# Two more input slots for the first batch, borrowed from tiles that are idle then, and a new order table

## The chip, the cores and the metric

The kernel runs on one core of one Trainium2 chip. The metric is device time in microseconds, the median of the runs shown. One execution was also taken by the hardware profiler; lines and durations in this text come from it.

## The reference

Two layers stand one behind the other, on four batches of 6272 steps and 256 channels.

```python
sig = 1 / (1 + exp(-f_logit))
f = lower_bound + (1 - lower_bound) * sig
for t in range(S):                       # S = 6272
    h = f[:, t] * h + (1 - f[:, t]) * x[:, t]
    y[:, t] = h
proj = y @ w_proj                        # 256 -> 3 * 256: x1, x2, x3
x2_conv = irfft(rfft(x2) * rfft(filter_fft))     # along t, circular, length S
out = (x1 * x2_conv * x3) @ w_out
```

The first is a gated recurrence, the second a long convolution between two gates. The filter's spectrum is the same for all batches and is made once.

## The kernel before

**An order written out.** No instruction is issued where the source names it. `op(...)` records an operation with the engines it may run on; `ORDER`, a table of packed entries, gives for each step the operation, its engine and its PSUM bank. `emit` goes through the table and issues. So the order on every engine, which engine evacuates what, and whether the third projection is copied or multiplied directly (`MUL`) all stand in the table. SP issues every DMA, in its table order: a DMA that waits holds back those behind it.

**Preparation (`prepare`).** The filter comes in 13 loads (`ff`, L610) of four rows each. A copy rounds them (`fr`, to a double buffer `afs`; ScalarE, GpSimd or VectorE), TensorE rotates them (`rot`, L621), and 26 evacuations (`f2`) write the filter's own layout. Meanwhile VectorE works out sine arguments (`args`), ScalarE takes two sines, and tables are cut from them. Then the filter's DFT: 32 matmul groups (`FF1`, L646) evacuated as `afs`, 16 groups (`FF2`, L664) evacuated as `hw` into a staging place, one last group (`last`) for the self-conjugate lines. From the staging place two DMAs for each pair of units (`hst`, L673; `hst2` and `hst3` are those of pair 1) store the spectrum in HBM. `hws` is the ring of places: three in `Hu`, two in `A`, two in `PP`, seven pairs' worth, for eight pairs.

**The recurrence (`hgrn`).** Thirteen chunks of 512 steps. A chunk's gate and input are loaded into slots of `FL` and `XT`, NX = 3 of each, in turn (`load`, L321). ScalarE takes a sigmoid (`sig`, L324), GpSimd multiplies (`u`, L326), TensorE turns both in two halves (`su`, L338), ScalarE or VectorE makes the gate (`f`, L351 or L353), VectorE scans (`scan`, L359). The first 3072 steps are copied behind the sequence as well (`wrap`, L293), since the convolution is circular.

**The rest.** `P` (L705) projects x2 once all scans and wraps of its batch are there. `F1`, `F2`, a product with the spectrum (`prod`, `pm`) and `I2` go through 16 units, four at a time. The gate (`x13`, L387, evacuated by `xs`) runs among them. At the end of a batch `I1`, `y`, `proj`, `o` and `store` make the output, with the next batch's recurrence among them. Some matmuls use 64 rows of the array (`su`, `F2`, `mini`, `I1`, `FF2`, `last`), the others 128.

**Places that the change touches.** `A` is 4096 columns of `HA`: scratch for the sine arguments at first, a staging place of the filter's spectrum next, and from the first `F1` on the ring of the DFT of the batches. `x1s` and `x3s` hold the gate's projections from the first `x13` on.

Of the kernel before, what the change touches and what calls it, by code (L numbers as in the profile page):

```python
# [9 lines left out]
F32 = mybir.dt.float32  # L10
# [49 lines left out]
class Plan:  # L60
# [63 lines left out]
    "AAYABIACIAOYA0gA5gA+gBIgBDgA1ABNgBSgBXgBcgBhgAxQAeQAhQAoQAcQAzYArQAPIAbQA6YBrgBmgA2QA4IA3AAQAA/YAmSBASBwgBJAA7UB"  # L124
    "BCBCCA8EAwWAlQD6gA9EBEYBFQBOYBGABKSBTYBMCARIBPUBQEBYIAUIBUWBdYBVOBRED5gBHIAqUASAADgBWGBZUBiYBaMBbEAkWBeWBLCEFgBj"
    "QBkABfGAWIATIERgBgGBlABsIAsSBnIBtSBoUEGgAVYAXYAYYAZYBxAB1YB2YBuCAfQByQB0ABzABvCBpMBqMB3QB4IB5SB+UB6KB7YD7AD8YCJQ"
    "B8SEHACOWB/MCAUCBECKIB9KCHQCIIETAESgCDUD9SCEMAFgCCYCPGCLYEBQCQWAEYD+CD/KECAEdgEIYCRGCSYEegEUYEDICMUCTWCNECUGEJSA"
    "aYEKKENUEOEEpgEqgELKEPMCZQCaACgWEVQEZSE1gEaKAHAE2gChGEbKCXWAIAEfAEgYCeUEWACYGCbYEXICcWAJACfECdOCiYCjSErAEsYEhQEl"
    "UFBgCkCEiIFCgEjIEmECuWALAEnMCvGE3AAnSCpSAMACqKEtQExWEuAFLgEvICnUE4YEyGFMgEzOCoECrYCwSGHgCsUCxCCyYFDAE5QE6IE9SE+K"
    "FVgFEYC5WE7IFWgCtEAKAEEYC6GC3UC4EEYYE/KCzWFNAFFUFIQFfgFJIC0GDASFGEFOYFKIFHMDBCC+WC/GC7YDCYC8SFggFXAFYYFPWFQOFROF"  # L130
    "SQFpgFqgDJUEcYC9CE0YFTAFUIDDSDKEDECDHUFhAFiYDIEDLYFZWFaOFbOFcSFzgF0gDQQFdCDRAFeKDOUDPEDSYCGgDMQDNIDTUFrAFsYCFgFj"
    "WEwYDUEFkGFlODeSDfCFmUAGgDXQF1AF2YF9gDYADZSDaCDbYFnMFoMDgWEQYDhGDiYFtQDcSFuAFvIF+gFwWDdCDGgMegFxGFyODpUDqEF3SF4C"
    "F5KDjQDkADwUDxMF6WF/AGAYF7GF8ODuQDvADnSDoCDrYDyYDFgGBUGCEEoYGDMDzQD0ADsSEkYCVgANAEAYC1gDtCDWgE8YClgGEWD3UGIgEMAG"
    "FOGGOMgAJbQJcRJgWJiGJdIJepJfYD4MJhXJlQJmRD1gJjPJoBJnIFAYGZSGaCGfUGgMGTWGUGGNQGOAJkYGPSD2gGQKGbUGXQGVSGJWGcMMqgGL"
    "UGYAGKGJpYMsAGRQCmgCWgGSAGWKGMMGdSGeCDmgC2gJqUJrVJsMJttJuYGhQGiAGtgJvWJwXJxOJyPJzYGjQGkAGnSGoCJ0UGlVJ2MGmNDlgJ1Q"
    "J5RJ3AJ4YGuSJ6QDVgGyqGzYG2gJ7BJ8AJ9YGwqGpUGqEJ+RKABJ/QKDTGxYGrUGsMGvYKFDG3WG7GG5uHRRKBoHSBKCYG/gKETG0UG1EKGrKHYH"
    "AWHCGHTQG8YHUAMfgHXUHEuHFYHJSG6YG4YHYEHIgG9WG+GHNqHOYHDYHVQHWAHKYKIUKJVHLqKNWKPGHBYKLNKOTKQDMrgHbgHGQMhYHZWHaOHc"
    "SHgqHeqHfYHMYKKEHHAHhYHlUHnEHkgKMYH/WIAGHdYHPQHmYHpsHoYHQAKSTKUDKRYKTUKVsIDWHuQIEGHiSHjCIBUICEHqYKXWKZGKYXHtgHyo"
    "HzYHwoHvYHxYMtYH2gKavKbYHrSH4YHsCIJgH3UH7sH5sH6YIFQIGAH0WM2gH1GH8YIKSIHQIIIILYIOCIMqKcVINYKeFITWIXGM4AKdTISgKfrH"
    "9QIPYH+AKhXIUYKjHIVuIbgItUIuEIWYIYYKiSKmTKoLIQQIRAIcWIeGKkqMiUIguM3gIkgIhYIlQMjEIpAMmSMnCMkMIdYI3gMoKIfYIZWIaGIm"  # L140
    "YInoKnRKppKqYNCgIqYJAgIvUIwENDgIiWIjGIxSIyCKlYMuUM5YMvMMwMIzWI0GIoYMyQNOgNPgNEAI4SI1WI2OI8CJBUKWYI5YI6qI7YMzAI9Y"
    "IrWJCYJJgNFYKrTKsSJSgJDEKtDM0IKwUIsGJFsJGYKyEKxTKzrKuqM6QM7AM8IM+WNagM/GK0YI+UI/EJEYK1TK3LK2SNQAJTUNRYNbgNGQJVEK"
    "6TNHANAOK7UJLYK8DNKWK4qK9sK+YKvYJXENIINLGJHSJYYJICJUYK/ULBELAVK5YLCFLDYNmgKgYNcANMOJKQJOoJPYNSSNngNWUNwgLEWNTCJM"
    "oLGGNdYJNYNXENUKNxgLFXLJRLLBLKWNoANpYLMuLNYLHvLIYNYMJQQLOSLPTJRALQCLRrLSYNeWNfGNgONZYNiQNjAN6gN7gLTSLVCLUULYVLZT"
    "R7SLWsJWYNyALXYNkILaFNqWNtUR9CNzYOEgLbrLcYNrGNsONuENvMR8SR+COFgJZQSATSBSJaALdQLeISDCSCDLiWN0UN3SOOgN8AN9YN4CM9AN"
    "JYLjOOPgN1EN5KN2MLfQOGAOHYLnWLoOLkSLgALhgMpYLlCLmgLsULtMN+QOBWOYgM1YLxSN/AOAIOCGODOOQAORYLpULqELrgOZgLuQLvALwgL2"
    "ULyKL3MOIWOJGOLQOigOjgOKOOMALzSL0CL1gONIOSUL7WL8OOTENBYOUMMlYOaAOVSOWCOXKL4QL5AL6gNVYNhgL9WMAUMBML+GL/gMFQMGIObY"
    "OcSOdCOeKOkAOfWOgGOhOU+gMCUOlYMxYMHQVKgMDEMEgOmSOnCOoKOpUOqEOrMVWgMPWMQOVXgNlAMIAMJgMKSMLKNNYOyUOzMO2QO3IU/gOwWO"
    "xGO4SO5KPAUPBMOsWO+QO/IVAAO8SO9KVMAOtGPCUPDMO6QO7AO0WO1OVYAOuSOvCVZYMMQPEUPFMMNAMOgMUWMVOMZSPGUPHEMRQMSAMaKSEYPK"
    "WPLOPQUPUsPVYPMSPNCVLgPSsPTYPogPIQPJAMWWSFSSGTMXGMYgPYQR/YSIDSHKPOUPPMPRYPcoPdYSJYPpWPgSPaoPbYPrGSKUP7gPiCPxVPZY"  # L150
    "SMEPWRPjYPkqPlYPhYPyFSLUSNsSPQPeVPsYPtuPuYPqYPXBSRAPfFQEgPzRP0BSQQSUTSSoSWLP1UP2EPmWPnGSVQSXoMTgP3RP4BQNgP8UPvWQ"
    "AsPwGVBYSYYP5QP6IP9YQGYP+sSOYP/YQFSQHCSZVQBYSbFQOWQSGQfQQgASaSQIYQJqQCUQTYQPYQXQQbASeTSfXSgDSjRQWgScqSlBQhSQiCQp"
    "gSdYQDMQQuQRYQKYSTYQLUQYYQcYQMESkRShvQjWQkGSmpQygQZoQaYQUSQqUQusQvYVNYSoRQVCSqBQssQtYQlWQmGQdSQeCSpQStRSroSsYSvB"
    "QnWQoOQ0YQrYQzUQ1sQ2YQ7gQ8SQ3EQ4YRFQREgQ+CRACSuVSwtQwWQ/YRBYQxGRJIRNSROKRXgVCUVGWVDEVjgVEMSyRVigVHGS0BVFgSzSS3TS"
    "4RSxYQ5UVIOS1CQ9YS5DS6BRggRPSQ6ERQCRHoS2YRIYVOWRKYVPOVQOSnYRRURSERCQS7YRYSRcqRDARpgS8URaqS+ERGYS9VS/FTAYRTQRUAVS"
    "WVvgVugVTGRhURVQRWIRdYRygRZYTBSVkAVlYTDCTCTTEDVUORLQTFYRlsRqWRMARuGRjsRmYVJgVaSRbYVbCVcKRkYReQRvYRfATGXVeUVmQV6g"
    "TIHRsuV7gRtYRiYVfEVgMVnAVoITHSTJCTLTTNDVqWWHgWGgVwARnSVrGTMUTOsRrYTKYRoCTQVTSFVxYTRQTVRTWSTTATUYV8AV9YVsOVhYRwUR"
    "zWTXJTYqSiYR1uRxEVyQV2SWQgVzAV0IWRgV3CV4KR3uR4YTaUTcETbVTfWTdFThGTgUTeYR2YV+QWCVWbgTZYTiETjYV/AWagV5gTkUTlSTpTR0"
    "YTqXWIAWJYTmEWAITnqTrDTsvTtYWDFV1gTuUTwER5QWENTvSTzTTxqTyYR6AT0UT4XToYT1DT2EMbQMcIMdgT5WT6HVdgT3YT9UWKQWLAWNSWOC"
    "WSAWTYTPYWkgT7uT8YT+MUCWUDOWPKT/UWlgWcAWdYWMIUAEUBgUEWUFGUHSUIKUGgUMUUNMWUQWVAWWIWXWWvgWYGWZOUJSWugUOUWmAUKCULgU"  # L160
    "RQUSIUPEWeSWhWWBYWnYVRYWfCWgKW4gWiGWjOW5gVtYabUadEacVUTQaeFUUAUWSUXKUbUUcMWwAWxYWoWWrQXDgWsAWtIagSahTaiCUYUWpGWq"
    "OajDW6AUgQUhIWySWzCUQgW0KVpYUZEUdWUlQUmIUVgUagW1UW2EW3MXCgUiSUqQUrIW7YUeGUfgVVgW8WUjCW/UdqgW9GW+OdegXAEXBMdrgXEA"
    "UnSWFYXFYUoCUsQXGWXHGXIOXJSXKCXLKd3gUkgUvUUwMUtAU0WU1OXOSXPCXMQXNIdfgdsAdtYXQUXRMXkSXlKdgAXaWXbOXcQXdIXUUXVEXiSX"
    "jKUugdhYXgWXhGXWQXXIXeUXfMXSSXTCXYQXZAUxWU5SU6KafYUpgd2gUyGUzgXsQXtAXoUXmSXpMakYXnCXqWXrOalQamRanAU2UaopapYXuSXv"
    "KX5YXxYd4AU3EU4gX4WX8uX9YXwQXyoXzYX0AX1YaqSYIgasCarTatDauYavRaxBX6uX7YYbgdiUdjEYTSYUCdkMdmQeDgeCgYAWdnAX2SYCuYDY"
    "YEGYFYX+UYKYYkgdoIX3CYBYX/EawXYRSYSCayva0Wa2OazYduUdyQdvEdzAa1Sa5TdwMa3Cd0Ia7DYGWYHGYVSYWCa4YYJUYLsYMYeOgYXWYYGd"
    "5YYNsYOYYtga6Qa+RbABa/SbBqbCYbDTYcWa8Aa9YYZQYaIYdYd6UeEAYeGYfYd7EYguYhYd8MbESbGCY2gYPQYmYbIWbJXbFDbHYbLPYQAbKGY/"
    "SYlUbMYYnsd+QZACeagYuWd/AYoYYyGYiSYvYYjCYzYbNUbOXbPEYpsZJgbQHYwuYxYePgZSgZBSZCCYqYYrUY4YYsEeAIY3WY7uY8YdlYZDSZEC"
    "Y5uZbgY0QY1AZFUdpYY6YeBgebgbRYbSXbUPbTSbVqbWYeFYd1YZGEY9QZHUZIMZLYZUYZKWZOOZPYZMuZkgZNYZTSZVqZWYZvUY+AeQAZwEZXqZ"
    "3gbXQbYRbcXZYYbZAeGUbeHbaBbdQbbYeHEbfAeIMZcWZQRZdYZgubgYZeGZfYaAgZhYZRBbhQbiTbjAbmWbnSecAbkrblYboGbpqbqYZtQZZUZm"  # L170
    "YedYZuAbrXbsWbuGZlSbtHbvYZaMZnqZzQZ0AZxUZyEZiWZpqaJgZ4QZoYZqYbwSZ8oZjGeRYbyCbxTbzDZ1UZ2MZ5YZ6oZ7YZ9YeKWemgaKReLG"
# [22 lines left out]
def kernel(  # L194
# [51 lines left out]

    FF1 = [("FF1", u, h) for u in range(NU) for h in range(2)]
    FF2 = [("FF2", u) for u in range(NU)] + ["FF2"]
    late = {}
    dram = ctx.enter_context(tc.tile_pool(name="dram", bufs=1, space=bass.MemoryType.DRAM))  # L250

    H = [dram.tile([2, M + 64, 2 * UE * 64], F16, name=f"H{u}") for u in range(NU // 2)]
# [695 lines left out]
```

## Time and profile before

| | |
|---|---|
| median of 3 runs | 465.07 us (464.01 to 465.59) |
| profiled execution | 461.81 us, span 460.0 us, granted clock 0.996 |
| first sigmoid, last sigmoid of batch 0 | starts at 25.70, ends at 69.56 us |
| last scan of batch 0 | ends at 73.04 us |
| first P of batches 0 to 3 | 75.2, 172.4, 273.4, 372.1 us |
| loads, stores | 121.67 MB, 264 GB/s over the span |

A stage boundary here is the start of the first matmul of line L705 in each batch. Busy shares are of one execution. Matmuls are pipelined, so a busy TensorE needn't be at its peak.

### The profile page before, as it was taken

What the parts mean: (1) busy time and instruction counts of PE and PEld (TensorE: products, weight loads), DVE (VectorE), ACT (ScalarE), POOL (GpSimd) and SP (SyncE); (2) the same over time, 40 slices, a digit from 0 to 9 for tenths busy, and PEclk for the clock granted to TensorE, in tenths of its full rate; (3) what the DMA queues carried; (4) which work ended last, traced back from release to release, by engine and by line L of the source; (5) the groups of instructions that cost most, each with busy time, mean ns of one, the idle gap of its engine ahead of it and who ended that gap; (6) DMA issues with size and microseconds to landing.
All of it is one profiled execution on the core that took longest, in us unless ns stands there. A gap on an engine that the chain in (4) does not pass through costs nothing.

```text
span 460.0 us, 14639 instructions
## 1 busy us (share of the span) xinstructions
PE 440.7 (96%) x6009; PEld 345.1 (75%) x6009; DVE 412.9 (90%) x472; ACT 399.7 (87%) x578; POOL 317.3 (69%) x299
## 2 busy tenths in 40 slices
PE   7798999999899999999999999999999999999998
PEld 5676778777766889777767889776768897777786
DVE  8689998789999999999999998999999957999972
ACT  4899998799899986889998985999999887899564
POOL 7698875197899840689997624689996522889600
PEclk9899999999999999999999999999999999999999
DMA  8978999877988897586887977578677832567276
GB/s 326 398 271 288 328 303 341 290 247 264 339 287 273 292 312 279 162 259 217 313 314 282 349 259 292 209 256 285 234 271 254 330 140 93 185 184 210 79 295 268
DMA packets 44531, 121.67 MB, mean 264 GB/s; under 512 B 4272, under 2 KB 6960, under 8 KB 44464
## 3 DMA queue, kind: packets, MB, share of 16 engines
q1 hardware_dynamic: 44464, 120.73, 74.6%
q8 instruction: 47, 0.77, 0.7%
q14 instruction: 20, 0.16, 0.1%
HBM read 87.69 MB, written 31.98 MB: 260 GB/s over the span
## 4 chain that ended last, share of the span: by engine, by line
PE 51%; DVE 12%; ACT 2%; issue 1%; DVEq 0%; ACTq 0%
PE PS L387 13%; PE PS L817 7%; PE PS L869 7%; PE PS L705 6%; DVE HA L359 5%; DVE ys L857 5%; PE PS L777 5%; PE PS L718 5%; PE PS L338 4%; PE PS L851 3%; DVE X L286 2%; PE PS L591 1%; ACT HA L281 1%; PE PS L734 0%; ACT Th L281 0%
## 5 line engine op out<-in xcount | busy, mean ns | idle before, releaser
L326 POOL TENSOR_TENSOR XT<-XT,FL 128x1024 f32<-128x1024 f32 (+1 forms) x52 | 116.9, 2250 | 55.6 <-ACT FL L324 40.6
L359 DVE TENSOR_TENSOR_SCAN HA<-fTs,HA,PS 128x512 f16<-128x512 f32 (+1 forms) x96 | 112.5, 1200 | 3.8 <-ACT fTs L351 3.3
L798 DVE TENSOR_TENSOR PP<-PS,Hu 98x1008 f16<-98x1008 f32 x87 | 101.4, 1197 | 3.8 <-PE PS L817 1.5
L387 PE MATMUL PS<-HA,W 128*128 128x490 f16 (+1 forms) x416 | 101.0, 367 | 1.2 <-ACT HA L281 1.1
L807 POOL TENSOR_TENSOR PP<-HA,Hu 98x1008 f16<-98x1008 f16 x41 | 86.2, 2108 | 3.4 <-ACT HA L281 3.2
L417 POOL TENSOR_TENSOR zt<-x1s,x3s 128x490 f16<-128x490 f32 (+1 forms) x48 | 58.4, 1224 | 37.3 <-DVE x3s L286 12.2
L281 ACT CAST HA<-PS 128x1024 f16<-128x1024 f32 (+1 forms) x95 | 78.5, 849 | 6.0 <-PE PS L718 3.1
L857 DVE TENSOR_TENSOR ys<-PS,zt 128x1024 fp32r<-128x1024 f32 (+1 forms) x52 | 58.7, 1154 | 11.8 <-PE PS L851 6.6
L351 ACT ACTIVATE fTs<-PS,nomc 128x512 f32<-128x512 f32 (+1 forms) x92 | 60.3, 673 | 5.2 <-PE PS L338 4.1
L283 ACT ACTIVATE osb<-PS 128x1024 f32<-128x1024 f32 (+1 forms) x51 | 49.8, 989 | 13.6 <-PE PS L869 9.2
L869 PE MATMUL PS<-Wo,ys 128*128 128x256 f32 x392 | 58.0, 292 | 2.6 <-DVE ys L857 1.9
L387 PEld LDWEIGHTS <-W 128*128 128x128 f16 x416 | 35.2, 97 | 31.7 <-issue 5.9
L817 PEld LDWEIGHTS <-PP 98*128 98x128 f16 x1024 | 48.7, 98 | 10.0 <-issue 2.7
L869 PEld LDWEIGHTS PS<-Wo,ys 128*128 128x128 f32 x392 | 49.3, 188 | 7.9 <-DVE ys L857 3.7
L281 ACT CAST Th<-PS 128x784 f16<-128x784 f32 x61 | 50.2, 828 | 4.3 <-PE PS L817 3.7
L324 ACT ACTIVATE FL<-FL 128x1024 f32<-128x1024 f32 (+1 forms) x52 | 52.8, 1025 | 1.3 <-DMA FL<-in_f_logit_dram 1.3
L817 PE MATMUL PS<-VA,PP 98*128 98x98 f16 x512 | 52.2, 207 | 0.2
L817 PE MATMUL PS<-VB,PP 98*128 98x98 f16 x512 | 51.9, 207 | 0.0
L283 ACT ACTIVATE x1s<-PS 128x490 f32<-128x490 f32 (+1 forms) x84 | 48.9, 591 | 1.3 <-DVE zt L408 0.5
L338 PE MATMUL PS<-iden,FL 64*128 64x64 f32 x784 | 44.9, 230 | 1.4 <-ACT osb L283 0.4
L705 PE MATMUL PS<-W,HA 128*128 128x256 f16 x392 | 44.9, 273 | 0.1
L705 PEld LDWEIGHTS <-HA 128*128 128x128 f16 x392 | 43.0, 142 | 1.4 <-issue 0.4
(114 smaller groups left out, 719.3 us busy)
## 6 DMA issues: line engine op xcount, KB each, us to landing
Hu<-H SPq DMA_DIRECT2D x55, 512.0 KB, 4.2
XT<-in_x_dram SPq DMA_DIRECT2D x48, 512.0 KB, 5.2
FL<-in_f_logit_dram SPq DMA_DIRECT2D x48, 512.0 KB, 4.9
out_dram<-osb SPq DMA_DIRECT2D x48, 512.0 KB, 3.9
X<-in_moe_filter_fft_dram SPq DMA_DIRECT2D x9, 512.0 KB, 7.2
H<-Hu SPq DMA_DIRECT2D x4, 512.0 KB, 5.9
Hu<-in_moe_filter_fft_dram SPq DMA_DIRECT2D x2, 512.0 KB, 9.7
H<-Hu SPq DMA_DIRECT2D x4, 256.0 KB, 6.4
```

The costliest lines, as they stand in the source:

```text
L281: nc.scalar.copy(dst, src)
L283: nc.scalar.activation(dst, src, AF.Copy, scale=scale)
L326: op("u", {"POOL": 0.1 + 0.553 * nb}, lambda e, xt=xt, ft=ft: nc.gpsimd.tensor_tensor(xt, xt, ft, op=AOP.mult), r=[("ft", k)], w=[("xt", k)])
L338: nc.tensor.transpose(bank(pb)[:, at[p] + j:at[p] + hn:nb], src[ps, j, cols], iden[ps, ps])
L359: nc.vector.tensor_tensor_scan(h, fT, bank(pb)[:, 512 - hn:512 + hn], init, op0=AOP.mult, op1=AOP.add),
L387: nc.tensor.matmul(PS[:, p, 0:n], W13[:, kh, js], HA[:, HB[kh] + t0:HB[kh] + t0 + n], start=(kh == 0), stop=(kh == 1))
L705: nc.tensor.matmul(pp[:, r - r0, :], column(HB[kh], q_of(r)), W2[:, kh, :], start=(kh == 0), stop=(kh == 1))
L798: nc.vector.tensor_tensor(pr, px.unsqueeze(1).broadcast_to([TB, 2, UE, 63]), hh, op=AOP.mult)
L807: nc.gpsimd.tensor_tensor(pr, spec[:, o, :, 1:64].unsqueeze(1).broadcast_to([TB, 2, UE, 63]), hh, op=AOP.mult)
L817: nc.tensor.matmul(PS[:, ib + o, pr * TB:(pr + 1) * TB], PP[:TB, k, o, n, 2 * pr:2 * pr + 2, :], v[:TB], start=(n == 0), stop=(n == 1))
L857: nc.vector.tensor_tensor(late["ys"][:, yk, :, 0:rn * 128], PS[:, cb:cb + 2, 0:rn * 128], late["zt"][:].rearrange("p k r m -> p k (r m)") ...
L869: nc.tensor.matmul(po[:, i, :], late["ys"][:, yk, kh, i * 128:(i + 1) * 128], Wo[:, kh, :], start=(kh == 0), stop=(kh == 1))
```

## The change

Batch 0 alone takes its chunks through five slots instead of three: chunk c goes to slot c mod 5. The two new slots are views, not new memory: slot 3 is `XS`, one tile that takes the place of `x1s` and `x3s` (and is 88 columns larger, so that a chunk fits), slot 4 is `A`, one half for the gate and one for the input. Since `A` is then taken, the ring of staging places for the filter's spectrum shrinks from seven to five. Four empty entries in the table (`pre`) tell the recorder when the borrowed tiles change hands; they issue nothing. Three small tiles are joined into one, `cols`. `ORDER` is new in every line; operations and their sizes are the same, and some change the engine.

```diff
-    late = {}
+    XS = konst.tile([128, 2048], F32, name="XS")
+    late = {k: XS[:, i * 1024:i * 1024 + 2 * XR * Q].rearrange("p (j n) -> p j n", j=2)
+            for i, k in enumerate(("x1s", "x3s"))}
...
+    more = [[v.rearrange("p (j d) -> p j d", d=D) for v in vs] for vs in (
+        [XS[:, i * 1024:(i + 1) * 1024] for i in range(2)],
+        [HA[:, A0 + i * 2048:A0 + (i + 1) * 2048].bitcast(F32) for i in range(2)],)]
+    more_t = (["xsf"] + [("x1s", j, i) for j in range(2) for i in range(2)],
+              [t for i in range(NA) for t in At(i) + Ax(i)],)
...
-            k = count["x"] % NX
-            count["x"] += 1
-            xt, ft = XT[:, k, 0:nb], FL[:, k, 0:nb]
+            if b == 0:
+                k = c % (NX + len(more))
+            else:
+                k = count["x"] % NX
+                count["x"] += 1
+            xt, ft = (more[k - NX] if k >= NX else (XT[:, k], FL[:, k]))
+            xt, ft = xt[:, 0:nb], ft[:, 0:nb]
...
-        hws += [(A[:, i * UE:(i + 2) * UE].rearrange("m (j i) r k -> m j (i r k)", j=2),
-                 [At(i + j) + Ax(i + j) for j in range(2)], []) for i in range(0, NA, 2)]
...
-        late["x1s"] = konst.tile([128, 2, XR * Q], F32, name="x1s")
-        late["x3s"] = konst.tile([128, 2, XR * Q], F32, name="x3s")
...
+        for i, t in enumerate(more_t):
+            op("pre", {"SP": 0.01}, lambda e: None, w=t + [("ft", NX + i), ("xt", NX + i)])
         hgrn(0)
+        for i, t in enumerate(more_t):
+            op("pre", {"SP": 0.01}, lambda e: None, w=t + [("ft", NX + i), ("xt", NX + i)])
```

The order of the first loads on SP behind the filter's 13 (f and x are gate and input, the number the chunk; W the projection's weights, wcol the lower bound):

```text
before  x0 f0 wcol f1 f2 x1 x2 W | f3 x3 f4 x4 f5 x5 ...
after   f1 wcol f0 f2 x0 f4 x1 W x2 f3 x3 x4 f5 Wo x5 ...
```

On ScalarE, ahead of the first sigmoid, 3 copies `fr`, 20 evacuations `f2` and 2 sines become 1, 19 and 2; GpSimd has 9 `fr` in place of 7.

## The prediction, made before the changed kernel was run

> **What bounds the kernel now.** I read the page first, then the stretches up to the first projection, then the order of time in the first 30 us, then the waits. The page:
>
> ```profile
> span 460.0 us, 14639 instructions
> ...
> PE 440.7 (96%) x6009; PEld 345.1 (75%) x6009; DVE 412.9 (90%) x472; ACT 399.7 (87%) x578; POOL 317.3 (69%) x299
> ...
> PE   7798999999899999999999999999999999999998
> ```
>
> TensorE idles 19.3 us in all, and the low digits stand in the first five slices, 57 us. By lines, the first projection (P, L705) starts at 75.2 us, and the four batches' projections start at 75.2, 172.4, 273.4 and 372.1. The change is aimed at what lies before 75.2, so I took the busy times of that stage, in equal stretches and then in the stretch that each engine's streaming work fills (columns: stretch, its length, busy PE, PEld, DVE, ACT, POOL, clock, DMA share, GB/s):
>
> ```profile
> 0.00:12.00 12.00, 8.79 (x56) 6.66 (x56) 10.13 (x37) 5.82 (x7) 9.10 (x23) 1.00 0.87 330
> 12.00:24.00 12.00, 9.03 (x50) 7.04 (x50) 7.94 (x13) 10.42 (x22) 8.92 (x14) 0.86 1.03 398
> ...
> 24.79:73.04 48.25, 44.81 (x594) 35.69 (x593) 45.68 (x47) 47.62 (x74) 39.78 (x44) 1.00 0.85 300
> 25.70:69.56 43.86, 40.43 (x554) 32.30 (x555) 41.50 (x41) 43.31 (x67) 36.67 (x38) 1.00 0.83 291
> ```
>
> From the first sigmoid (25.70) to the last (69.56) ScalarE works 43.31 of 43.86 us: it sets the pace, one chunk in about 3.4 us. VectorE is next, 45.68 of 48.25 us from its first `afs` to its last scan. Ahead of that ScalarE is far from full, and the order of time shows what holds the first sigmoid:
>
> ```profile
> 10.14 1.04 POOL L293 CAST afs<-X 128x1024 fp32r<-128x1024 f32 x1 [1.40 <-PE PS L621]
> 12.09 1.16 POOL L293 CAST afs<-X 128x1024 fp32r<-128x1024 f32 x1 [0.92 <-PE PS L621]
> ...
> 19.09 3.39 ACT L281 CAST f<-PS 128x512 fp32r<-128x512 f32 x6 [1.43 <-DVE f L286]
> ...
> 22.62 1.77 ACT L281 CAST f<-PS 128x512 fp32r<-128x512 f32 x4
> 24.41 1.28 ACT L324 ACT_TABLE_LOAD   x1
> 25.70 2.01 ACT L324 ACTIVATE FL<-FL 128x1024 f32<-128x1024 f32 x2
> ...
> 26.85 2.39 POOL L326 TENSOR_TENSOR XT<-XT,FL 128x1024 f32<-128x1024 f32 x1 [0.49 <-ACT FL L324]
> ...
> 30.33 0.33 SPq L321 DMA_DIRECT2D FL<-in_f_logit_dram  x1
> ```
>
> The filter's copies (`fr`, L293) wait for the rotation before, the evacuations `f2` end at 24.4, the table is loaded, and only then does the first sigmoid run. The last line is the fourth chunk's load: with three slots SP issues none between 19.6 and 30.3. The transfers land one in 1.28 us up to then (the filter's twelfth at 18.74, its last at 19.11, the next input at 20.38).
>
> **The change part by part.** An op with a number below is the op's place among its kind in program order.
>
> *The slots alone.* What they could remove is waiting for inputs. In the whole trace ScalarE waits 1.3 us for `FL`, and up to 75 us GpSimd waits 0.2 us for `XT`. Earlier loads are thus worth between 0 and 1.5 us; I take 0, since both chunks' inputs have been there when the full engine comes to them. What is left is the order that they permit.
>
> *Ahead of the first sigmoid.* The old order has ScalarE do 3 `fr`, 20 `f2`, 2 sines; the new one 1, 19 and 2. Nine `fr` in place of seven go to GpSimd in a row, so the waits of up to 1.40 us between them should shrink to the landings. ScalarE's evacuations follow the first sine directly: 19 at 0.55 us from start to start (eight in 4.42 us) and one sine, 0.68, from about 8.5 end at 19.6 if nothing stops them. The landings stop them: the twelfth group lands at 18.74, its copy takes 0.69, rotation 0.74, evacuation 0.66, so 20.9; with the table's 1.28 the first sigmoid is at 22.2. The late end is 25.7, if the waits stay. SP's new order brings the gate of chunk 1 first, in the place that lands at 20.38, so it doesn't bind. I take 22.9, nearest the landings: 2.8 us earlier. The x of chunk 0 has gone back to the place that landed at 25.57, so GpSimd's first product starts there in place of 26.85, 1.3 us earlier, and it loses nothing, as it has room (below).
>
> [...] The scaling of the arguments took 1.27 us at 4.65 (L508, 520 columns) beside GpSimd's copies and 0.42 us at 11.5 without; two GpSimd copies took 1.38 us on average in 5.98 to 8.74, later ones 1.04. So nine copies beside VectorE's sines cost between 0 and 9 x 0.34 = 3.1 us more. I take 0: copies now end on landings, and GpSimd is idle 2.9 us in the first 12. [...]
>
> *Sigmoids to the last scan.* Counted from the first sigmoid to the last, with the rows' durations: ScalarE has 9 fewer `afs` (0.59 each), 3 more `f` (0.69), 2 more `hw` (1.03), 2 more `xs` (0.59): 50.04 us before, 49.99 after, in sums that overlap by the factor 43.31/50.04. So its 43.3 us stay, and its last sigmoid is at 22.9 + 43.6 = 66.5. VectorE, from its first `afs` to its last scan: 8 more `afs` (0.68), 2 fewer `hw` (1.21), 3 fewer `f` (0.72), one `f2`, one `xs`: 48.02 becomes 50.16, or 45.68 becomes 47.7 us busy. Its start follows the filter's last evacuation, 24.8 - 2.8 = 22.0, so its end is 69.7 with no idle time and 72.3 with the 2.57 us of now. GpSimd, first to last product: 37.85 becomes 39.13 by one more copy `wrap` (0.61) and one `z` (1.23) less two small ones; from 25.6 it could be done by 65, in front of the last sigmoid.
>
> *From the last sigmoid to P.* Now: last sigmoid 69.56, last product 70.43, last scan 73.04, and five `wrap` copies of the state, the last at 74.87, since they stand behind it on GpSimd; P at 75.2. In the new order four are behind the last product with two small copies, 4 x 0.61 + 2 x 0.2 = 2.9 us, and one went to SP, in front of it. By ScalarE then P is at 66.5 + 0.9 + 2.9 = 70.3; by VectorE at 70 to 72.6. I take 71.5, between: 3.7 us earlier. Bounds 70.2 and 75.2.
>
> *Behind P.* The last filter matmul (0.56) moves behind P with its evacuation, one x13 pair (0.42) moves ahead: +0.1. All other TensorE instructions are the same in number and shape. Its turns between 64-row and 128-row kinds fall from 194 to 186 after the first P; F1 then F1 takes 0.45 us from start to start, F1 then F2 0.54, so a turn costs 0.1 and eight save 0.8. In the stages from the first I1 to the next P, where VectorE is the chain, its rows add 0.1, 0.5 and 0.5 us: +0.9 at the overlap of now. Sum 0.2, taken as 0. The uncertainty is larger: batches 0 to 2 hold the same TensorE work and take 97.2, 101.0 and 98.7 us from P to P, a scatter of 1.9, so three re-drawn ones scatter by 3.3.
>
> *Sum.* The profiled execution took 461.81 us for a span of 460.0; 461.8 - 3.7 = 458.1. It lies 3.3 below the median of the runs, 465.07, so the forecast against that is 461.4.
>
> **The rivals.** *The filter stage gains nothing (time 464.6).* VectorE, which gets the 2.1 us more, or the GpSimd copies take the place of ScalarE: P at 74.7. For it: VectorE now idles only 2.57 of 48.25 us. Against: its start moves too.
>
> *Staging places are the new wait (slower, 466.6).* Spectra took seven places in turn, now five, so `hw10` to `hw15` write where an earlier pair is still to be stored. In the new SP queue the stores of pair 1, `hst2` and `hst3`, stand behind the store `hst11`, which needs `hw11`, and a load that needs chunk 7 transposed. From `hw11` to `hw12` ScalarE has 13 ops: six `f`, three sigmoids, two `afs`, two `xs`, 9.7 us by rows, 8.4 with the overlap. SP needs about 1.9 us for the four issues (intervals 0.4 to 0.7 at 58 us), and stores landed 4.0 to 6.5 us after issue: ready 8.4 us after `hw11` at the late end. It is even, then. Beyond that each us is lost on the full engine, with sigmoids and the load queue behind it. The trace's longest landing is 10.9 us, 4.4 more; on top of VectorE's late end (P at 72.3) P is at 76.7: 465.1 + 1.5 = 466.6. Alone it decides from 5.1 us of waiting at `hw12` (3.7 + 1.4), more than the landings explain.
>
> *The re-drawn batches lose it (slower, 467.4).* Periods of 101.0, batch 1's, for the two others cost 3.8 + 2.3 us, against the 3.7. For it: the scatter. Against: sums and turns are equal or less.
>
> *The slots don't come in time.* The first extra load could stand behind something late. In the order of SP it is sixth behind the filter's, in a place issued before 19 us, so I give this nothing of its own; it would end in the first rival.
>
> **How the numbers follow.** About 0.3% (1.4 us) is what a measurement of this kernel tells from no change. The forecast's case, a gain over 1.4 us, gets 0.60; no gain in the filter stage 0.16; staging places 0.12, the batches 0.12, both slower. Predicted 461.4. The low end is P at its bound (5.0) and batches better by 3.6: 456.5. The high end takes in both slower cases, 466.6 and 467.4: 467.5.
>
> **What would show it.** Right: first sigmoid near 22.9, the last near 66.5, P near 71.5, ScalarE still full in between, last scan not over 72; P to P between 97 and 101. Wrong: ScalarE waits over 1 us ahead of `hw10` to `hw13` for a store; VectorE without a gap while ScalarE idles; GpSimd's `fr` copies over 1.2 us each; or P early and the batches longer by as much, which would void the sum.

## The result, and the profile after

The changed kernel is slower: 468.26 us median (465.92 to 470.65, four runs) against 464.54 for the kernel before in the same session. The ratio is 1.0118 with a 95% interval of 1.0072 to 1.0164; it is estimated from the single runs, and the two medians alone divide to 1.0080. Measured again beside other kernels (the run e8 below) it stood at 1.0065 [1.0022, 1.0109], 467.75 us. Both intervals exclude a gain. Runs over 1.5% above the fastest of their kernel are left out of every ratio, and of the times by clock further down. The profiled execution took 465.93 us for a span of 463.8.

A word for what follows: a *filler* is a `warm` operation of the kernel (L591 before, L599 after), four matmuls on the identity whose result nobody reads. Both kernels have 24 of them; the order table decides where they stand.

The page of the changed kernel, the same lines as were shown of before, and the clock's row of the 40 slices:

```profile
span 463.8 us, 14640 instructions
...
PE 440.4 (95%) x6009; PEld 346.6 (75%) x6009; DVE 412.0 (89%) x477; ACT 400.9 (86%) x574; POOL 310.9 (67%) x285
...
PE   8689989899999999999999999999999999999997
...
PEclk9889999999999999999999999999999999999999
```

TensorE's busy time is the same as before within 0.3 us. The span grew by 3.8 us of idle time, and the low digits stand in the second slice and the last. The stages in the two profiled executions:

| us | before | after |
|---|---|---|
| first sigmoid starts | 25.70 | 25.71 |
| last sigmoid of batch 0 ends | 69.56 | 72.33 |
| last scan of batch 0 ends | 73.04 | 76.70 |
| first P of batches 0 to 3 | 75.2, 172.4, 273.4, 372.1 | 77.0, 173.7, 274.1, 373.3 |
| last projection matmul ends | 456.5 | 458.0 |
| end | 460.0 | 463.8 |

So 1.8 us are lost ahead of the first P, 0.3 are won from there to the last projection, and 2.3 are lost behind it. The busy times of the same stretches as before (stretch, its length, busy PE, PEld, DVE, ACT, POOL, clock, DMA share, GB/s):

```profile
0.00:12.00 12.00, 10.00 (x63) 7.60 (x64) 10.17 (x35) 7.52 (x11) 9.97 (x25) 1.00 0.87 334
12.00:24.00 12.00, 7.36 (x36) 5.38 (x34) 9.56 (x15) 7.92 (x15) 11.65 (x18) 0.86 1.01 392
...
25.30:76.70 51.40, 47.68 (x597) 37.41 (x596) 47.21 (x53) 48.56 (x74) 40.52 (x42) 0.97 0.90 325
25.71:72.33 46.62, 42.90 (x562) 34.18 (x561) 42.73 (x47) 43.79 (x65) 37.56 (x36) 0.96 0.89 332
```

Between 12 and 24 us ScalarE works 7.92 us (10.42 before) and TensorE 7.36 (9.03 before), while GpSimd went from 8.92 to 11.65. From the first sigmoid to the last ScalarE works 43.79 us, near the 43.31 of before, but in 46.62 us in place of 43.86: it is no longer full. The order of time shows what ScalarE waits for:

```profile
13.90 1.04 POOL L295 CAST afs<-Hu 128x1024 fp32r<-128x1024 f32 x1 [0.23 <-DMA Hu<-in_moe_filter_fft_dram]
...
18.17 3.61 ACT L283 CAST f<-PS 128x512 fp32r<-128x512 f32 x6 [2.02 <-DVE f L288]
...
23.75 0.65 ACT L283 CAST f<-PS 128x512 fp32r<-128x512 f32 x1 [1.06 <-DVE f L288]
24.42 1.28 ACT L336 ACT_TABLE_LOAD   x1
25.71 2.95 ACT L336 ACTIVATE FL<-FL 128x1024 f32<-128x1024 f32 x3
...
26.66 0.20 POOL L663 CAST mX<-afs 128x16 fp32r<-128x16 f32 x1 [2.19 <-DVE afs L288]
28.07 0.21 POOL L663 CAST mX<-afs 128x16 fp32r<-128x16 f32 x1 [1.20 <-DVE afs L288]
28.24 2.38 POOL L338 TENSOR_TENSOR XT<-XT,FL 128x1024 f32<-128x1024 f32 x1
```

GpSimd's copies do run closer, with 0.23 us in place of 1.40 ahead of one. But ScalarE's evacuations now wait 2.02 us for VectorE's, and the first product waits behind two small copies `mX` that GpSimd's queue has in front of it. VectorE is late because of its sine arguments. The last three operations of the second set, before (L508 to L510) and after (L516 to L518), each kernel in its own fence:

```profile
11.48 0.42 DVE L508 TENSOR_SCALAR PP<-HA 128x512 f32<-128x512 f32 x1
11.93 0.43 DVE L509 TENSOR_SCALAR PP<-PP 128x512 f32<-128x512 f32 x1
12.39 1.41 DVE L510 TENSOR_TENSOR PP<-HA,PP 128x512 f32<-128x512 f32 x1
```

```profile
11.81 0.96 DVE L516 TENSOR_SCALAR PP<-HA 128x512 f32<-128x512 f32 x1
12.81 1.15 DVE L517 TENSOR_SCALAR PP<-PP 128x512 f32<-128x512 f32 x1
13.99 1.50 DVE L518 TENSOR_TENSOR PP<-HA,PP 128x512 f32<-128x512 f32 x1
```

The whole set takes 8.4 us (7.04 to 15.48) in place of 5.4 (8.36 to 13.80). Seven of GpSimd's nine filter copies fall beside it, three of seven before. Last, the clock. Taken from edge to edge of the half-clock windows, the stretch from 15.8 us reads so in the changed kernel, and the one such window of before so:

```profile
15.80:19.20 3.40, 1.36 (x10) 0.90 (x9) 2.98 (x5) 1.38 (x3) 3.40 (x5) 1.00 1.03 398
19.20:22.60 3.40, 3.29 (x13) 2.57 (x12) 1.66 (x3) 3.04 (x6) 3.40 (x7) 0.50 0.97 356
22.60:26.00 3.40, 1.66 (x13) 1.49 (x12) 1.88 (x5) 2.31 (x4) 1.87 (x5) 1.00 1.04 420
26.00:29.40 3.40, 3.40 (x16) 2.93 (x16) 2.49 (x5) 2.70 (x4) 1.54 (x3) 0.50 1.03 413
```

```profile
11.90:15.30 3.40, 1.69 (x10) 1.25 (x10) 2.00 (x3) 3.40 (x8) 2.21 (x2) 1.00 1.02 407
15.30:18.70 3.40, 3.23 (x15) 2.64 (x16) 2.33 (x5) 2.21 (x4) 1.41 (x2) 0.50 1.04 405
```

A window of 3.41 us at clock 0.50 follows each stretch in which TensorE was busy 1.4 to 1.7 of 3.4 us. The changed kernel has two, the kernel before one.

The other end, ScalarE's last three evacuations of projections in the changed kernel:

```profile
455.45 1.03 ACT L285 ACTIVATE osb<-PS 128x1024 f32<-128x1024 f32 x1 [0.80 <-PE PS L877]
456.84 1.02 ACT L285 ACTIVATE osb<-PS 128x1024 f32<-128x1024 f32 x1 [0.37 <-PE PS L877]
459.63 0.38 ACT L285 ACTIVATE osb<-PS 128x256 f32<-128x256 f32 x1 [1.76 <-DMA out_dram<-osb]
```

The last one waits 1.76 us for the store of an earlier piece to land, so that its buffer comes free. Before, it waited for TensorE's last projection:

```profile
456.57 0.38 ACT L283 ACTIVATE osb<-PS 128x256 f32<-128x256 f32 x1 [1.13 <-PE PS L869]
```

### The profile page after: what moved, and what is told of

The parts are those of the page before. It is cut to its first block, busy times and chain, and to the rows that moved or that the text cites. A ratio compares the mean times of both kernels' runs of the same rounds, so it can differ in the third digit from the quotient of the medians.

```text
span 463.8 us, 14640 instructions
## 1 busy us (share of the span) xinstructions
PE 440.4 (95%) x6009; PEld 346.6 (75%) x6009; DVE 412.0 (89%) x477; ACT 400.9 (86%) x574; POOL 310.9 (67%) x285
## 4 chain that ended last, share of the span: by engine, by line
PE 57%; DVE 19%; ACT 8%; issue 6%; DMA 5%; POOL 4%; DVEq 0%; ACTq 0%; POOLq 0%
PE PS L399 13%; PE PS L713 7%; PE PS L877 7%; PE PS L825 7%; DVE HA L371 6%; PE PS L350 5%; PE PS L726 5%; PE PS L785 4%; DVE ys L865 4%; PE PS L859 4%; DMA Hu<-H 4%; PE PS L654 2%; DVE PP L806 2%; ACT HA L283 2%; POOL XT L338 2%
## 5 line engine op out<-in xcount | busy, mean ns | idle before, releaser
L338 POOL TENSOR_TENSOR XT<-XT,FL 128x1024 f32<-128x1024 f32 (+1 forms) x48 | 107.5, 2241 | 56.7 <-ACT FL L336 47.9
L815 POOL TENSOR_TENSOR PP<-HA,Hu 98x1008 f16<-98x1008 f16 x51 | 107.1, 2104 | 14.4 <-ACT HA L283 10.7
L806 DVE TENSOR_TENSOR PP<-PS,Hu 98x1008 f16<-98x1008 f32 x77 | 90.7, 1197 | 4.8 <-PE PS L785 1.7
L285 ACT ACTIVATE XS<-PS 128x490 f32<-128x490 f32 (+1 forms) x96 | 55.7, 589 | 2.7 <-PE PS L399 1.2
L283 ACT CAST Th<-PS 128x784 f16<-128x784 f32 x60 | 49.0, 821 | 4.7 <-PE PS L825 4.2
L420 DVE TENSOR_TENSOR zt<-PS,XS 128x490 f16<-128x490 f32 (+1 forms) x78 | 50.0, 651 | 3.1 <-ACT XS L285 1.1
L336 ACT ACTIVATE FL<-FL 128x1024 f32<-128x1024 f32 (+1 forms) x48 | 48.3, 1014 | 4.0 <-DMA FL<-in_f_logit_dram 4.0
L429 POOL TENSOR_TENSOR zt<-XS 128x490 f16<-128x490 f32 (+1 forms) x26 | 31.7, 1221 | 25.8 <-DVE ys L865 24.5
```

The costliest lines, as they stand in the source:

```text
L283: nc.scalar.copy(dst, src)
L285: nc.scalar.activation(dst, src, AF.Copy, scale=scale)
L338: op("u", {"POOL": 0.1 + 0.553 * nb}, lambda e, xt=xt, ft=ft: nc.gpsimd.tensor_tensor(xt, xt, ft, op=AOP.mult), r=[("ft", k)], w=[("xt", k)])
L806: nc.vector.tensor_tensor(pr, px.unsqueeze(1).broadcast_to([TB, 2, UE, 63]), hh, op=AOP.mult)
L815: nc.gpsimd.tensor_tensor(pr, spec[:, o, :, 1:64].unsqueeze(1).broadcast_to([TB, 2, UE, 63]), hh, op=AOP.mult)
```

## The experiments

Three things were to be told apart: the stage ahead of P (contention, queues, clock), the new order behind P, and the end. All runs are timed against the kernel before on the same chip; "P to end" is of the profiled execution, and the clock is the mean of the granted clock over all runs of that kernel (0.9967 for the 142 runs of the kernel before). Most kernels have 10 or 12 runs, e6 four, e15 and e16 six.

| run | ratio [95%] | first P | P to end | clock |
|---|---|---|---|---|
| before | 1 | 75.2 | 384.8 | 0.9967 |
| e1 two copies to ScalarE | 1.0028 [0.9993, 1.0062] | 75.5 | 388.7 | 0.9928 |
| e2 fillers in gaps | 1.0038 [1.0004, 1.0071] | 74.8 | 385.4 | 0.9956 |
| e3 products first | 1.0039 [0.9996, 1.0082] | 75.2 | 387.6 | 0.9915 |
| e4 stores later | 1.0065 [1.0029, 1.0101] | 72.7 | 389.2 | 0.9936 |
| e5 slots, old order | 1.0012 [0.9976, 1.0049] | 74.6 | 385.7 | 0.9973 |
| e6 new rest | 1.0138 [1.0084, 1.0192] | 79.3 | 388.4 | 0.9952 |
| e7 new part ahead of P | 1.0064 [1.0033, 1.0096] | 80.7 | 384.4 | 0.9918 |
| e8 changed, again | 1.0065 [1.0022, 1.0109] | 80.4 | 386.2 | 0.9907 |
| e9 end of before | 1.0055 [1.0023, 1.0088] | 76.4 | 386.4 | 0.9909 |
| e10 before, 4 fillers moved | 1.0085 [1.0054, 1.0115] | 78.2 | 387.3 | 0.9899 |
| e11 gaps and end | 1.0026 [0.9994, 1.0058] | 74.1 | 386.3 | 0.9985 |
| e12 all together | 1.0047 [1.0013, 1.0081] | 74.8 | 387.3 | 0.9941 |
| e13 gaps, old rest | 0.9996 [0.9964, 1.0029] | 75.0 | 388.9 | 0.9968 |
| e14 early P, old rest | 0.9980 [0.9953, 1.0007] | 74.0 | 387.8 | 0.9978 |
| e15 joint in another bank | 1.0101 [1.0058, 1.0143] | 72.9 | 391.2 | 0.9915 |
| e16 the same, copies to ScalarE | 1.0090 [1.0058, 1.0123] | 74.0 | 391.2 | 0.9907 |
| e17 last group ahead of P | 0.9997 [0.9969, 1.0026] | 76.4 | 385.4 | 0.9966 |

**One part at a time.** The diffs are of the order table, one operation a line.

```diff
 e1
-GpSimd   fr:4, fr:6
+ScalarE  fr:4, fr:6
 e2  (bank 6; four of them taken from between the last projections, one from behind them)
+TensorE  2 fillers before rot:8, 3 fillers before FF1:0
 e3
+SP       load:3 behind load:8 (in the table alone; SP's own order stays)
+GpSimd   u:1 before mX:2; rest:2 behind u:2
 e4
+SP       hst:5, hst:9, hst:11 behind load:25
```

> The changed kernel with two of the filter's nine GpSimd copies (fr 4 and 6) given to ScalarE; nothing else. In the changed kernel the second set of sine arguments on VectorE took 8.44 us (5.44 before), beside GpSimd copies that ran back to back, and the evacuations behind it were late. Theory 'contention': the arguments take 0.57 us less per us of copy taken away, so about 7.2 us; the first sigmoid moves from 25.7 to about 24.6, the first P from 77.0 to about 76.0, the time by -1. Rival 'the arguments are slow for another reason': they stay at 8.4 and the first sigmoid at 25.7 or later.

The second set of arguments took 6.2 us in place of 8.4 (7.2 expected by the theory) and ended at 13.2 in place of 15.5. The first sigmoid came at 25.4 all the same (24.6 expected), and P at 75.5, with two half-clock windows still (16.9 and 23.8).

> The changed kernel with five of the eleven filler matmul groups (warm) from its end put into TensorE's gaps: two ahead of rotation 8 (idle 16.2 to 16.8), three ahead of the first filter DFT group (idle 22.7 to 24.5). The trace of the changed kernel shows two windows of 3.41 us at half clock (from 19.2 and from 26.0), that of before one (from 15.3); the changed kernel's runs fall into two groups, 465.9 us at a granted clock of 0.993 and 470.6 at 0.985 to 0.989, as with two, three and four such windows. Theory 'idle TensorE drops the clock': one window at most, clock 0.993 or higher in every run, no run near 470.6, first P about 1 to 1.5 us earlier, median about 465. Rival 'windows come from elsewhere': clocks and both groups stay.

One window in place of two, P at 74.8. The arguments still ended at 15.5: TensorE's gaps were filled and VectorE's delay left, so the windows hang on the first. The lowest clock of its runs is 0.993, and none took over 467.1 us, as the theory has it. The ratio isn't the windows' alone, though: from the first I1 of batch 3 to the end it takes 26.7 us (28.5 in the changed kernel), since no filler stands between the last projections any more. Even so the last evacuation waits 1.04 us for a store.

> The changed kernel with the product of chunk 1 (u 1) ahead of two small copies (mX 2 and 3) on GpSimd, and the table ID (rest 2, 1.83 us) behind the product of chunk 2 in place of ahead of it. Theory 'GpSimd's queue holds the chunks back': u 1 from 32.7 to 30.6, u 2 from 36.9 to about 33, scans 3 us earlier at first; P earlier by 1 to 2.5 us, as ScalarE and VectorE take up their idle time. Rival 'ScalarE sets the pace anyway': u 1 and u 2 earlier, P the same within 0.5 us.

GpSimd's third product came at 31.9 in place of 36.9 us, the last sigmoid ended at 70.5, and P came at 75.2, 1.8 us earlier. This execution had one half-clock window where the changed kernel's had two, so not all of the 1.8 need be the products'.

> The changed kernel with three stores of the spectrum (hst 5, 9 and 11, 256 KB each), which no staging place waits for soon, behind the last load of batch 0 on SP. In the changed kernel ScalarE waits 1.60 us at the sigmoid of chunk 11 for its gate, which landed 8.5 us after issue, and VectorE (1.7) and TensorE (2.0) wait behind it. Theory 'stores among the loads': the wait goes, P 1.5 us earlier. Rival 'the loads are late since their slots come free late': the wait stays over 1 us.

The wait at the sigmoid of chunk 11 is gone, as the first theory has it, and P is the earliest of all with the new rest, 72.7. Yet the ratio is 1.0065: from P to the end it took 389.2 us. A window came at 11.1 us, ahead of the stage; in this execution the arguments ended at 13.8 us, 1.6 us before those of the changed kernel, though nothing differs ahead of there. No one part is shown to bring the kernel back to before (the intervals of e1 and e3 just reach 1, and all four overlap that of e8), and the stage ahead of P doesn't decide the time alone.

**Code against order, and the two halves of the order.** e5 has the changed code (five slots, five places) with the order of before; only SP's loads stand two chunks earlier, and stores that the fewer places need are drawn forward. e6 and e7 join the two orders at the first P.

```diff
 e5
-ORDER of after
+ORDER of before, load:6 to load:9 behind the last filter load, later loads two chunks earlier
 e6  ORDER of before up to P, of after behind it
 e7  ORDER of after up to P, of before behind it
 e8  no edit
```

> The five slots and the five places for spectra alone: the changed code with the order table of before, in which only SP's part differs: the loads of chunks 3 and 4 stand behind the last filter load, each later one two chunks earlier, and the stores of spectra that the five places need done are drawn forward behind the loads. Theory A (the loss lies in the new order ahead of the first P): as before, first sigmoid 25.2 to 26, first P 74.5 to 75.5, ratio to before 0.998 to 1.002. Theory B (the places for spectra or the loads that come earlier cost time by themselves): ScalarE waits over 0.5 us ahead of a spectrum or a sigmoid, P at 76 or later, ratio 1.003 or more. If the slots are worth something without a new order, P comes before 74.5.

Near theory A's numbers: first sigmoid 25.0, P 74.6, ratio 1.0012, in an execution without any half-clock window. So no cost and no gain of slots and places can be seen within the interval, and the new order is left as what costs.

> Before up to the first P (its slots and its order), the new order behind it. Theory A (the loss lies ahead of P): P at 75.2 as before, the end as before, 460 to 461 for the span at full clock, ratio 0.998 to 1.002. Theory C (the new order behind P loses by itself, 2.3 us of it between the last projection matmul and the end): last projection to the end 5.1 to 5.9 us where before has 3.5, span 462 to 463, ratio 1.004 to 1.007.

> The changed kernel up to the first P (five slots, new order), the order of before behind it. Theory A (the loss lies ahead of P): first sigmoid 24.3 to 25.7, P at 75.5 to 77, span 461 to 462.5, ratio 1.003 to 1.008; last projection to the end 3.5 us as before. Theory C (the new order behind P loses): P between 72.5 and 77 as the runs so far gave it, and the end at that of before or ahead of it, ratio 0.994 to 1.002.

Both joints were badly made. What one order has ahead of P and the other behind it came to stand right in front of P: in e6 16 filler matmuls and the gate's groups (last scan 73.1, P 79.3), in e7 24 filler matmuls (2.78 us) and the last filter group (last scan 76.2, P 80.7). Their ratios and P say nothing. What can be read lies behind P: 388.4 us with the new rest, 384.4 with the old. That speaks for theory C, but one pair of executions doesn't show it: the last projection to the end took 4.8 us in e6, under the 5.1 to 5.9 of the theory, and e10 below, with the old rest, takes 387.3 from P to the end.

> The changed kernel itself, beside the others on the same chip. If its ratio to before belongs to the kernel and not to the chip or to single runs: 1.008 to 1.015, granted clocks of 0.985 to 0.993 in most of its runs, first P at 76 to 77.5. If the one profiled execution was an unlucky one: first P at 72.5 to 75.5 and a ratio of 1.003 to 1.008, like that of the three kernels that change a few places of the new order.

In this execution of the same kernel one half-clock window of 10.24 us stands at 20.5 us and one of 3.41 at 71.7, and P comes at 80.4. Over its 10 runs the granted clock lies between 0.982 and 0.996, six of them at 0.993 or less. So a loss belongs to the kernel. Its ratio lies under the first range and inside the second, but the one profiled execution was no unlucky one: P has come at 77.0 and at 80.4.

**The cause of the windows, and of the end.**

```diff
 e9   changed kernel, from I1:0 of batch 3 on the order of before
 e10  kernel before:
-TensorE  fillers between rot:6 and rot:12 (4 fillers, 16 matmuls)
+TensorE  the same fillers behind the last projection
 e11  e9 and e2
 e12  e11, e1, e3, e4
```

> The kernel before with four of its fillers (16 matmuls of 128x256) taken from between the rotations, 14 to 23 us, and put behind the last projection; nothing else moves. Clock theory (the half-clock windows come where TensorE is left idle between 12 and 24 us, as the new order leaves it): two windows or one of 10 us between 15 and 30 us, mean granted clock of the runs 0.985 to 0.993 in place of 0.996 to 1.0, first P at 76 or later, ratio 1.003 to 1.01. Rival (the windows come whatever TensorE does there, and the loss is VectorE's arguments beside GpSimd's copies): clocks as before, first P 74.5 to 75.7, ratio 0.998 to 1.002.

This is the run that settles where the windows come from. Nothing but 16 matmuls whose result nobody reads was moved, in the kernel before, and the mean clock fell to 0.9899 and the ratio rose to 1.0085, as slow as the changed kernel. P came at 78.2. Its windows:

```profile
12.50:15.90 3.40, 1.33 (x8) 1.06 (x8) 1.96 (x6) 3.40 (x7) 1.07 (x2) 1.00 1.02 406
15.90:19.30 3.40, 2.95 (x11) 2.28 (x11) 2.75 (x5) 2.60 (x5) 1.82 (x3) 0.50 1.04 405
19.30:22.70 3.40, 2.46 (x11) 2.20 (x11) 1.97 (x5) 2.88 (x6) 3.40 (x7) 0.50 1.03 377
22.70:26.10 3.40, 2.70 (x12) 2.26 (x11) 1.29 (x2) 3.20 (x8) 3.40 (x6) 0.50 1.02 414
26.10:29.50 3.40, 3.40 (x18) 3.01 (x16) 2.07 (x3) 2.79 (x3) 1.89 (x4) 0.50 0.53 207
```

TensorE is busy 1.33 of 3.40 us, and then four windows at half clock follow, up to the first one in which it is busy throughout. Not all of the 5.5 us between the two profiled executions (465.5 against 460.0) are the windows': the second set of arguments began 1.0 us later here, ahead of the first filler that was moved, and 1.3 us more pass behind the last projection. There the last evacuation waits for a store, with the order of before:

```profile
461.31 0.38 ACT L283 ACTIVATE osb<-PS 128x256 f32<-128x256 f32 x1 [1.77 <-DMA out_dram<-osb]
```

> The changed kernel with the order of before from the first I1 matmul of batch 3 on (projections, evacuations, stores and the fillers between them). Tail theory (the fillers that the new order puts between the ninth, tenth and eleventh projection delay the evacuation whose store must land before the last evacuation may write): last evacuation waits for TensorE and not for a store, last projection to the end 3.3 to 4.2 us where the changed kernel has 5.5 to 5.8, first I1 of batch 3 to the end 1.5 to 2.3 us shorter, ratio to before 0.004 lower than that of the changed kernel. Rival (stores land later in the new kernel because of what else moves): last projection to the end stays over 5 us.

> Both parts: five fillers of the end moved into TensorE's gaps ahead of the eighth rotation and of the first FF1, and from the first I1 of batch 3 on the order of before. If clock and tail are the whole loss: first P 74.5 to 76, last projection to the end 3.3 to 4.2 us, clocks 0.993 to 1.0, ratio 0.997 to 1.003. If the new order ahead of P loses by itself: ratio 1.004 or more.

In e9 the last evacuation waits 1.13 us for TensorE and no longer for a store; from the first I1 of batch 3 to the end it takes 27.3 us (26.4 before; 28.5 in the changed kernel, 28.2 in e8). That is 1.2 us shorter and not 1.5 to 2.3, and the ratio is 0.001 under that of e8 and not 0.004. Last projection to end is 4.5 us, a little over the range, since its last store landed 2.5 us after issue and not 2.0. In e11 this end takes 26.7 us and there is no half-clock window before the last store; its runs have 0.996 to 1.0. TensorE in the stage that had the windows, and ScalarE's last two evacuations:

```profile
12.00:24.00 12.00, 9.15 (x64) 7.36 (x64) 8.80 (x15) 9.44 (x16) 12.00 (x17) 1.00 1.02 398
24.00:36.00 12.00, 11.81 (x132) 9.70 (x130) 11.18 (x16) 11.99 (x16) 9.71 (x12) 1.00 1.03 408
```

```profile
454.49 1.02 ACT L285 ACTIVATE osb<-PS 128x1024 f32<-128x1024 f32 x1 [0.81 <-PE PS L877]
456.64 0.39 ACT L285 ACTIVATE osb<-PS 128x256 f32<-128x256 f32 x1 [1.13 <-PE PS L877]
```

With both parts the ratio is 1.0026 [0.9994, 1.0058], where the changed kernel had 1.0065 and 1.0118; its interval holds 1. But at full clock P is at 74.1, only 1.1 us ahead of before, which had one window, and 0.5 ahead of e5, which has the old order and none.

> Both parts of the run with gaps and tail, and besides the fifth and seventh filter copy on ScalarE, products ahead of the next small copies on GpSimd, and the stores of pairs 2, 4 and 5 behind the loads. If the gains add: first sigmoid 23.5 to 24.5, first P 71.5 to 73.5, ratio 0.990 to 0.997. If, as in the run with later stores, the batches give back what is gained ahead of P: first P 71.5 to 73.5 with 387 us or more from there to the end, ratio 0.998 to 1.002.

P at 74.8, not at 71.5 to 73.5: the gains ahead of P don't add. This execution had a window at 16.0 us, and the first sigmoid came only at 26.6.

**Is the new order worth anything, once mended?** The next runs join the new part ahead of P, with its gaps filled, to the order of before behind P.

```diff
 e13  e2's fillers; order of before behind P (one filler, not four, between the last projections); mX:15, last:0, hw:16 behind the first P groups
 e14  e13, e3, e4
 e15  e14; last:0 in bank 0; 1 filler before rot:6 and 1 before rot:7
 e16  e15, e1
 e17  e15, but last:0 (with mX:15) before scan:25 and hw:16 behind it, ahead of P; x13:6 in bank 6
```

> The changed kernel up to the first P with five fillers in TensorE's gaps (as in the runs with gaps), and behind it the order of before, with the fillers that are left over at the very end. If the new order behind P loses by itself: first P 74 to 75.5, from there to the end 384 to 386 us as in before, batch 3 from P to I1 61.5 us, ratio 0.996 to 1.001. If the batches give back any gain ahead of P, whatever their order: from P to the end 386 us or more, ratio 1.001 to 1.004.

> The same with the stores of pairs 2, 4 and 5 behind the loads and the products ahead of the next small copies on GpSimd, which is to bring P forward: first P 72 to 74. If the new order behind P loses by itself: 384 to 386 us from P to the end, ratio 0.991 to 0.997, faster than both kernels. If the batches give back any gain: 387 us or more from P to the end, ratio 0.999 to 1.003.

The ratios, 0.9996 and 0.9980, are those of the kernel before; e13's lies in the first theory's range and e14's between the two. The times from P to the end, 388.9 and 387.8 us, speak for the second theory, but batch 0's own stage from P to I1, right at the joint, has 74.9 and 73.9 of them (73.1 before).

> As the run with early P and the old rest, with the last filter matmul in a bank that is free earlier and two more fillers between the rotations. If the joint cost it: batch 0 from P to I1 72.3 to 73.3 us, first P 72.5 to 74, from P to the end 385 to 386.5 us, ratio 0.993 to 0.997, clocks 0.996 to 1.0. If the batches give back any gain: from P to the end 387.5 us or more, ratio 0.998 or more.

> The same with the fifth and seventh filter copy on ScalarE. If the copies beside VectorE's arguments still cost something: the arguments end at 13 to 14 us in place of 15.4, first P 0.5 to 1.5 us earlier than in the run with the mended joint. If not: the arguments end earlier and P stays within 0.5 us.

P came at 72.9, with no window ahead of it. But the bank I gave to the last filter group came free late, and the group (L690) and the P groups behind it waited:

```profile
84.33 0.56 PE L690 MATMUL PS<-mX,FTr 64*98 64x128 f32 x8 [1.31 <-ACT X L283]
87.51 1.87 PE L713 MATMUL PS<-W,HA 128*128 128x256 f16 x8 [2.62 <-DVE X L288]
```

```profile
83.10:86.50 3.40, 0.56 (x8) 0.59 (x9) 1.50 (x2) 1.08 (x2) 0.00 (x0) 1.00 0.95 297
86.50:89.90 3.40, 2.39 (x10) 1.57 (x10) 2.09 (x2) 0.49 (x1) 0.00 (x0) 0.50 0.65 227
89.90:93.30 3.40, 3.40 (x19) 2.07 (x18) 2.01 (x3) 1.97 (x3) 0.26 (x1) 0.50 0.24 89
```

Waits of 3.9 us brought two half-clock windows of themselves, here in the middle of the kernel: batch 0 took 79.2 us from P to I1. It is the effect of e10 at another place. e16's arguments ended at 13.7 us in place of 14.6, and its P came no earlier (74.0, with a window at 11.1 us).

> Early P, seven fillers in TensorE's gaps, the order of before behind P, and the last filter matmul with its evacuation ahead of P as in before. If the gain ahead of P is kept when nothing waits at the joint: first P 72.5 to 74.5, batch 0 from P to I1 72.3 to 73.3 us, from P to the end 384.5 to 386.5 us, clocks 0.996 to 1.0, ratio 0.992 to 0.997, faster than both kernels. If the batches give it back: from P to the end 387.5 us or more, ratio 0.998 to 1.003.

With the last group ahead of P the time from P to the end is 385.4 us, as the first theory has it, but P is at 76.4 in this execution, and the ratio is 0.9997. No version was found that is measurably faster than before; e14 comes nearest.

## Why the prediction was wrong, point by point

*The slots alone, taken as 0.* Right as far as it can be seen: e5, 1.0012, with P 0.6 us earlier in an execution that lacks before's half-clock window.

*Ahead of the first sigmoid, 25.7 to 22.9.* Wrong, and the step that failed is the cost of nine copies beside VectorE, which I put at 0 out of 0 to 3.1 us. The second set of arguments alone took 3.0 us longer. Over 12 executions of orders with nine copies on GpSimd it took 6.8 to 8.9 us, with the order of before 5.2 to 5.5 (before, e5, e6, e10), with two copies on ScalarE 6.2 to 6.7 (e1, e12, e16). The prediction's reason, that GpSimd had 2.9 us of room and copies end on landings, looked at GpSimd's time. The copies indeed got no slower (six in a row took 6.27 us, 1.04 each); the price was paid by VectorE, and by ScalarE that waited for it. I had the landings stop ScalarE's evacuations at 20.9 us; they ended at 24.4, with 3.3 us of waits for those of VectorE. That the 3.0 measured lie beside the 3.1 I had as a bound is luck, as those 3.1 were a price of slower copies. At full clock, in two single executions, the first sigmoid is 0.6 us ahead of the old order's and P 0.5 (e11 against e5), where I had 2.8 and 3.7. By what a copy on GpSimd slows VectorE no run shows. That the contention alone keeps the first sigmoid at 25 us is not shown either: with the arguments at 13.2 to 13.7 it came at 25.2 to 26.6, with two copies on ScalarE.

*The clock.* It had no term in the sum. The row of before that I quoted for 12 to 24 us has 0.86 in its clock column, and TensorE 9.03 of 12 us. I read idle TensorE time as harmless while ScalarE set the pace, and never asked how near that stage was to a second window. The new order takes TensorE's work there to 7.36 us, with one filler between 12 and 24 us where before has four, and the late VectorE adds gaps. In the runs of the kernel before, those at clock 1.0 take 462.2 us on average (60 runs), at 0.996 463.5 (48), at 0.993 464.5 (25): 1.2 us for each window. The changed kernel's 13 runs (the first four and e8) have a mean clock of 0.9912 against 0.9971, 1.6 windows more, so by that price about 1.9 us of the 3.9 by which the means differ. At one window (0.996) its four runs still take 464.5 against 463.5, so the windows are not the whole loss. e10 and e11 show from both sides where the windows come from; the price is read from runs that differ in clock, and no run fixed the clock by itself.

*Sigmoids to the last scan.* The sums were right: ScalarE 43.79 us (43.3 said), VectorE 47.21 (47.7 said). What failed is that ScalarE stays full. 1.6 of its 2.8 us idle time is one wait for an input that I held to be safe, the gate of chunk 11: issued at 56.32, landed at 64.78, among stores of spectra. "GpSimd could be done by 65" fell with its queue: the last product ended at 73.1, and `mX` copies waited 6.3 us in all, ahead of products. I had counted 0.2 us for each of them, and not what stands behind them.

```profile
POOL mX L663 <- DVE afs L288: 5.1, 4, 2.2
...
ACT FL L336 <- DMA FL<-in_f_logit_dram: 1.6, 1, 1.6
...
POOL mX L663 <- ACT afs L283: 1.2, 2, 1.0
```

*From the last sigmoid to P.* The one mechanism that came: with wraps moved forward P follows the last scan by 0.3 us, by 2.2 before. The gain of 1.9 us is in the result, under 3.7 us of a later last scan.

*Behind P, 0 net.* Right for the periods (96.7, 100.4, 99.2 us from P to P; sum 296.3, before 296.9), wrong for batch 3, which has no period. From P to I1 it takes 61.7 to 63.1 us in ten executions with the new order, 62.3 on average, and 61.4 to 61.6 in nine with that of before; what makes it longer was not tested. From that I1 to the end it takes 2.1 us more in this pair of executions, 27.8 us on average in the seven with the new end and 26.8 in the twelve others, so about 1. I counted the matmuls and never laid the two ends side by side. The store that the last evacuation waits for is issued 3.4 us ahead of the last projection's end, with three of the fillers in between, and lands 4.86 us later; before it is 4.3 us ahead, with four fillers in between, and lands 3.95 us later. With the order of before from I1 on, the wait is gone in e9, e11 and e12. But the fillers' places alone are not shown to be the cause: the wait stays with none of them there (e2, 1.04 us), and in e10 it comes with the order of before, where that store lands 4.76 us after its issue. Why stores land later stays open.

*The rivals.* "The filter stage gains nothing" is nearest for the stage, for the reason it names (the copies and VectorE), but it ended at 464.6 without clock and end. Staging places did not wait: 0.04 us at `hw12`. "The re-drawn batches lose it" had the sign and the side, not the place: 467.4 by periods, where it was the end. The range ended 0.8 us under the result; each of its slower cases had one loss alone, and here several came together.

## What to carry to other kernels

Before a stage is re-ordered, look at TensorE's busy share there in steps of the clock's window (3.41 us in these traces), also where TensorE is not the bound: matmuls whose result nobody reads may be what holds the clock (with 16 of them moved in e10 the mean clock was 0.9899, and 0.9967 without the move), and an order that drops them pays for it outside of every sum of durations. A copy given to an idle GpSimd is to be priced on VectorE (here the second set of arguments took 8.4 us beside seven copies and 5.4 beside three), and a small operation put in front of others in a queue by the latest of what it waits for. Read the last stage of the kernel op by op, since it has no cover and no period that would show it.

## What the runs showed of the hardware that I had not expected

TensorE's half clock comes in windows of 3.41 us or whole multiples (6.83, 10.24, 13.65), at a granted clock of 0.50, on a raster whose phase differs from execution to execution (a window starts at 15.3 us before, at 19.2 and 26.0 in the changed kernel, at 20.5 in e8). In 17 of the 19 profiled executions there are 22 rows of such windows before the last store. The stretch of 3.41 us ahead of a row had TensorE busy for 16% (e15) to 65% (e14), in 20 of the 22 cases for 57% or less; up to the last projection no stretch under 48% went without one, some of 49 to 66% did, and none of over two thirds had one. Each row ended behind a window with TensorE busy for 88% or more; behind nine windows with 53 to 93% it went on. So one kernel has a different number of windows from run to run with nothing changed in it (granted clocks of 0.982 to 0.996 in the ten runs of e8), and a single profile of such a stage tells little. The longest single gap ahead of a window in the filter's stage was 2.63 us (e10), in the profiled execution of the changed kernel 1.74, in e14 0.52, so by the traces short gaps can be enough: ahead of the window of e14 they are 0.24, 0.44 and 0.52 us, 1.2 us in all.
